# Agent attention and gated feed-forward in one kernel: fixed places for the values, denser keys, a column for eps

## The chip, the cores and the metric

The kernel runs on one core of a Trainium2 chip. The metric is the device time of one execution in microseconds. Engines: TensorE (PE, matmuls; PEld is its weight load), VectorE (DVE), ScalarE (ACT), GpSimd (POOL) and SyncE (SP), which here issues all DMA transfers. Each engine works through its own queue in order and waits on semaphores.

## The reference

```python
def _attn_ref(q, k, v, agents):            # B, N, C = 4, 12480, 128; 49 agents
    scale = 1.0 / np.sqrt(q.shape[-1])
    def sm(a, b):
        s = scale * (a @ b.transpose(0, 2, 1))
        s = s - s.max(-1, keepdims=True)
        e = np.exp(s)
        return e / (e.sum(-1, keepdims=True) + 1e-09)
    a2k = sm(agents, k)
    agent_v = a2k @ v
    q2a = sm(q, agents)
    return (q2a @ agent_v).astype(np.float32)

def _moe_ref(x, w_in, w_out):              # 49920 tokens, 128 -> 2048 -> 128
    h = x @ w_in
    g = h * (1.0 / (1.0 + np.exp(-1.702 * h)))
    return (g @ w_out).astype(np.float32)
```

The output is `_moe_ref(_attn_ref(q, k, v, agents))`. In each batch 49 agents attend to 12480 keys and collect values, the 12480 queries attend to the agents, and each token's result goes through a feed-forward layer with a hidden width of 2048.

## The kernel before, in words

**Two parts.** For a batch the kernel first works out `agent_v` and folds it into the first feed-forward matrix: `avT` times `w_in` gives weights `wh`, `wl` (high and low part) of 128 by 2048, of which the agents fill the rows (`weights_sums`, `weights_part`). After that a token needs only its softmax over the agents, the *pairs* `sa`, `sb` (a high and a low part stacked), as the moving operand of the up matmuls.

**Steps and groups.** A group is 960 tokens (2 halves of 480); a batch has 13 groups, four batches 52. A group takes NF = 16 steps, one for each 128 of the hidden width, so there are 832 steps. In step t = 16 n + f:

- `up` makes four matmuls of 480 columns (L386, L388) into two PSUM banks of a ring of four, and ScalarE applies the gated activation to both halves (L391) into `g`;
- the jobs that are listed for this step, below;
- `high_low` makes `gh` (L398 on ScalarE for the steps in HI_ON_ACT, L400 on VectorE for the other eight) and `gl` = g - gh (L401, VectorE);
- `down` makes six matmuls (L412) of step t - LAG, LAG = 4, from `gh` and `gl` of that step into `po`; after step 15 of a group `store` copies `po` (L423) and sends it out.

So TensorE is at step t while `gl` of t - 4 is the latest that it needs.

**Jobs.** A table `at` holds for every step the functions to run there, in the order in which `put` was called. For the query group n + 1, during group n: scores at step Q_AT = 4 (32 small matmuls L177 to L180, reduced by VectorE at L184), shift by the maximum at 5 (L341, L342), exponential at E_AT = 7 (ScalarE, with a table load before and after), sums at 9 (L351 reduce, L352 adds eps, L353 reciprocal), softmax at 10 (L358), transposes and pairs at P_AT = 13 (L369, L374 to L377); the load of group n + 2 at 5 and its split into three bf16 parts on GpSimd (L163, L164) at S_AT = 14.

For the next batch, during this one, 13 key groups and 13 value groups:

- *keys*: load 13 steps ahead, split 6 ahead (GpSimd, L163 and L164), scores at step t (as for a query; `score` holds them), partial maximum at t + 1 (L223). They come every 6 steps in the first batch, every 7 in the others. Then the maximum over all keys (`key_max_0` to `key_max_2`, two transposes on TensorE);
- *values*: subtract the maximum (GpSimd, L263), exponential with the query's at step 7 of some group (L267), two or three key groups at a time; at t - 2 `key_pair` (ScalarE L272, GpSimd L273) and `value_hi` (VectorE L276); at t - 1 `value_lo` (VectorE L280); at t eight matmuls `key_values` (L284); at t + 1 VectorE adds the result (L301). They come every 7 steps;
- *weights*: sums, then four parts (L324 to L326).

`pe_step` moves a job of TensorE to the next step that holds none. All these small jobs share a ring of two PSUM buffers, `ps_m`: a third one waits until the first has been read.

**Order.** The steps run inside `tc.manual_schedule` for TensorE, ScalarE, VectorE and GpSimd: on these engines the instructions stand in the order of the program. What lies before the loop (all of the first batch's keys and values, the conversion of the first weights) is ordered by the scheduler. In group 0 the last three quarters of `w_out` are still converted from 64-bit words (`down_weights`, L119 to L141) at steps 1, 5 and 9.

```python
        slot = next(t for t in range(shift + 3, steps) if t % NF == E_AT)
        t = slot + 3
        for k in range(NKG):
            t = pe_step(t)
            ...
            put(t - 2, lambda k=k: key_pair(k))
            put(t - 2, lambda b=b, k=k: value_hi(k, vts[b + 1, k]))
            put(t - 1, lambda b=b, k=k: value_lo(k, vts.pop((b + 1, k))))
            put(t, lambda b=b, k=k: do_key_values(b + 1, k))
            put(t + 1, lambda b=b, k=k: do_key_sum(b + 1, k))
            last, t = t, t + 7
```

Of the kernel before, what the change touches and what calls it, by code (L numbers as in the profile page):

```python
# [8 lines left out]
F32 = mybir.dt.float32  # L9
F32R = mybir.dt.float32r  # L10
# [7 lines left out]
P = 128  # L18
TB = 120
# [3 lines left out]
LAG = 4  # L23
RED = 1
PAD = 8
SD = 2
Q_AT = 4
E_AT = 7
P_AT = 13
S_AT = 14  # L30
FIRST_WORDS = (1, 3, 5, 7)
FIRST_UP = (0, 2, 4, 6)
HI_ON_ACT = (0, 2, 5, 6, 10, 12, 13, 14)
EPS = 1e-09


# [1 line left out]
def kernel(  # L38
# [47 lines left out]
    for i in range(2):  # L86
# [7 lines left out]
        nc.gpsimd.memset(t, 0.0)  # L94
        p_pad.append(t)

    w_in_sb = const.tile([P, F], F32, name="w_in_sb")
    wo_h = const.tile([P, NF, C], F32R, name="wo_h")
    wo_l = const.tile([P, NF, C], F32R, name="wo_l")
# [47 lines left out]
    for i in range(3):  # L147
        nc.vector.tensor_copy(out=ag_part[:, :, i, :], in_=rest)
        if i < 2:
            ag_rest = work.tile([P, B, A], F32, name="ag_rest", tag="sd", bufs=SD)  # L150
            nc.vector.tensor_sub(out=ag_rest, in0=rest, in1=ag_part[:, :, i, :])
            rest = ag_rest

# [177 lines left out]
        nc.sync.dma_start(out=t[:, 0:GT], in_=qT[b, :, g * GT : (g + 1) * GT])  # L331
        return t

    def query_scores(b, parts):
        sd = work.tile([P, KB, A], F32, name="sd", bufs=SD)
        scores(b, parts, sd[:TB])
        return sd

    def query_shift(sd):
        m = work.tile([P, KB], F32, name="m")  # L340
        nc.vector.tensor_reduce(out=m[:TB], in_=sd[:TB], axis=AX.X, op=ALU.max)  # L341
        nc.vector.tensor_tensor(  # L342
            out=sd[:TB], in0=sd[:TB], in1=m[:TB].unsqueeze(2).broadcast_to([TB, KB, A]), op=ALU.subtract
        )

    def query_exp(e):
        nc.scalar.activation(out=e[:TB], in_=e[:TB], func=AF.Exp, scale=scale)

    def query_sums(e):
        z = work.tile([P, KB], F32, name="z")  # L350
        nc.vector.tensor_reduce(out=z[:TB], in_=e[:TB], axis=AX.X, op=ALU.add)  # L351
        nc.vector.tensor_scalar_add(out=z[:TB], in0=z[:TB], scalar1=EPS)  # L352
        nc.vector.reciprocal(out=z[:TB], in_=z[:TB])  # L353
        return z

    def query_softmax(g, e, z):
        pp = p_pad[g % 2]
        nc.vector.tensor_tensor(  # L358
            out=pp[:TB].rearrange("p i (c x) -> p c i x", c=2)[:, :, :, 0:A],
            in0=e[:TB].rearrange("p (c i) a -> p c i a", c=2),  # L360
            in1=z[:TB].rearrange("p (c i) -> p c i", c=2).unsqueeze(3).broadcast_to([TB, 2, KB // 2, A]),
            op=ALU.mult,
        )
# [17 lines left out]
    def up(f, wts, pairs):  # L381
        wh, wl = wts
        s = slice(f * P, (f + 1) * P)
        ph = [ps_h.tile([P, 512], F32, name="ph") for _ in range(2)]
        for c in range(2):
            nc.tensor.matmul(out=ph[c][:, :CH], lhsT=wh[:, s], rhs=pairs[c], start=True, stop=False)  # L386
        for c in range(2):
            nc.tensor.matmul(out=ph[c][:, :CH], lhsT=wl[:, s], rhs=pairs[c], start=False, stop=True)  # L388
        g = gpool.tile([P, 2, CH], F32, name="g")
        for c in range(2):  # L390
            nc.scalar.activation(out=g[:, c, :], in_=ph[c][:, :CH], func=AF.Gelu_apprx_sigmoid)  # L391
        return g

    def high_low(f, g):
        gh = gpool.tile([P, 2, CH], F32R, name="gh", bufs=LAG + 1)
        gl = gpool.tile([P, 2, CH], F32R, name="gl", bufs=LAG + 1)
        if f in HI_ON_ACT:
            nc.scalar.copy(out=gh, in_=g)  # L398
        else:
            nc.vector.tensor_copy(out=gh, in_=g)  # L400
        nc.vector.tensor_sub(out=gl, in0=g, in1=gh.bitcast(F32))  # L401
        return gh, gl
# [66 lines left out]
    def do_query_scores(n):  # L469
        if n < B * NG:  # L470
            b, g = divmod(n, NG)
            scored[n] = query_scores(b, q_parts.pop(n))

    def do_query_shift(n):
        if n < B * NG:
# [5 lines left out]

    def do_query_sums(n):
        if n < B * NG:
            sums[n] = query_sums(scored[n])

    def do_query_softmax(n):
        if n < B * NG:
# [6 lines left out]


    def first_keys():
        tags = [("g", 3), ("gh", LAG + 1), ("gl", LAG + 1)]
# [129 lines left out]
    E = mybir.EngineType  # L627
    live = {}
    po = {}
    with tc.manual_schedule(engines={E.PE, E.Activation, E.DVE, E.Pool}):  # L630
        for t in range(steps + LAG):
            if t < steps:
                n, f = divmod(t, NF)
                g = up(f, wts[n // NG], pairs[n])
                if f == NF - 1:
                    pairs.pop(n)
            for job in at.pop(t, ()):
                job()
            if t < steps:
                live[t] = high_low(f, g)  # L640
            if t >= LAG:
                n, f = divmod(t - LAG, NF)
                if f == 0:
                    po[n] = [ps_o.tile([P, 512], F32, name=f"po{c}") for c in range(2)]
                down(f, live.pop(t - LAG), po[n])
                if f == NF - 1:
                    store(*divmod(n, NG), po.pop(n))
    assert not at


# [36 lines left out]
```

## Time and profile before

| | us |
|---|---|
| median of 3 runs | 2275.52 |
| lowest and highest run | 2273.99, 2277.99 |
| the profiled execution | 2273.38 |
| its span, first to last instruction | 2271.6 |

The mean granted clock of TensorE in the span was 0.972 of full speed. In rows of groups the columns are: line, engine, operation, output and inputs, shapes, count, then busy time, mean ns of one, and the idle time before them with what ended it. In rows of the timeline: start and duration in us, engine, line, operation, and in brackets the engine's idle time before with its releaser. In rows of waits: engine and line, what it waited for, us in total, times, longest. In rows by stretch: the stretch and its length, then for PE, PEld, DVE, ACT and POOL the busy time with the count of instructions, the granted clock, the share of the DMA engines and GB/s.

### The profile page before, as it was taken

Reading aid. Unit: us, or ns where it says so; the run is one execution under the profiler, and the core shown is the slowest. Engines: PE = TensorE matmul, PEld = TensorE weight load, DVE = VectorE, ACT = ScalarE, POOL = GpSimd, SP = SyncE. Lnnn points to the kernel's source line nnn. Section 1 sums busy time; section 2 is a strip of 40 time slices with the busy share of each in tenths; the row PEclk is TensorE's granted clock in tenths of the full one; section 3 lists DMA queues with packets and bytes.
Section 4 is the critical chain, followed back from the end, with each engine's and each line's share of the span. In section 5 each row is a group of like instructions: output and inputs, shape, how many; then the busy total and the mean of one; then the engine's idle time right before and its main releaser. Section 6 shows DMA issues by size and latency. Waiting matters only on the chain.

```text
span 2271.6 us, 31765 instructions
## 1 busy us (share of the span) xinstructions
PE 2126.4 (94%) x12232; PEld 1810.4 (80%) x12232; DVE 1918.7 (84%) x2142; ACT 1578.6 (69%) x2560; POOL 530.3 (23%) x383
## 2 busy tenths in 40 slices
PE   8789988897999999898899999989889999999999
PEld 8578877776788888776778888877677888888887
DVE  6799988877889999878788999978778888888876
ACT  3377766675677777666667777766576878787876
POOL 3144322211213333232122333232212101111000
PEclk9899999999999999999999999999999999999999
DMA  9312111211111111111111111111110010101000
GB/s 259 95 53 68 49 42 35 61 35 44 44 36 53 53 54 44 53 44 35 44 44 44 44 62 53 46 43 44 44 35 28 26 33 21 36 18 36 18 18 18
DMA packets 49339, 108.57 MB, mean 48 GB/s; under 512 B 4252, under 2 KB 30172, under 8 KB 49188
## 3 DMA queue, kind: packets, MB, share of 16 engines
q1 hardware_dynamic: 49188, 106.55, 15.9%
q8 instruction: 96, 1.57, 0.3%
q14 instruction: 55, 0.45, 0.1%
HBM read 80.97 MB, written 25.56 MB: 47 GB/s over the span
## 4 chain that ended last, share of the span: by engine, by line
PE 75%; DVE 16%; ACT 5%; issue 3%; DMA 1%; POOL 0%; ACTq 0%; SPq 0%; DVEq 0%; POOLq 0%
PE po L412 40%; PE ph L386 13%; PE ph L388 13%; DVE gl L401 6%; DVE v_pair L280 3%; PE ps_m L284 3%; DVE gh L400 3%; ACT g L391 2%; ACT gh L398 1%; PE ps_m L177 1%; PE ps_m L200 1%; PE ps_m L179 1%; PE ps_m L369 1%; PE ps_m L324 1%; PE ps_m L178 1%
## 5 line engine op out<-in xcount | busy, mean ns | idle before, releaser
L391 ACT ACTIVATE g<-ph 128x480 f32<-128x480 f32 x1664 | 855.6, 571 | 569.3 <-PE ph L388 494.0
L401 DVE TENSOR_TENSOR gl<-g,gh 128x960 fp32r<-128x960 f32 x832 | 1096.2, 1323 | 179.7 <-ACT gh L398 162.0
L412 PE MATMUL po<-gh,wo_h 128*128 128x480 f32 x1664 | 525.9, 398 | 0.0
L412 PE MATMUL po<-gh,wo_l 128*128 128x480 f32 x1664 | 507.7, 387 | 0.0
L412 PE MATMUL po<-gl,wo_h 128*128 128x480 f32 x1664 | 506.1, 386 | 0.0
L398 ACT CAST gh<-g 128x960 fp32r<-128x960 f32 x416 | 415.0, 997 | 12.2
L400 DVE CAST gh<-g 128x960 fp32r<-128x960 f32 x416 | 334.8, 805 | 74.0 <-ACT g L391 73.4
L412 PEld LDWEIGHTS po<-gl,wo_h 128*128 128x128 f32 x1664 | 319.6, 192 | 52.6
L412 PEld LDWEIGHTS po<-gh,wo_l 128*128 128x128 f32 x1664 | 318.9, 192 | 51.4
L412 PEld LDWEIGHTS po<-gh,wo_h 128*128 128x128 f32 x1664 | 304.9, 193 | 44.8 <-issue 5.7
L386 PE MATMUL ph<-sa,wh 128*128 128x480 f32 x832 | 321.2, 386 | 10.6 <-ACT g L391 10.5
L386 PE MATMUL ph<-sb,wh 128*128 128x480 f32 x832 | 320.1, 385 | 0.5 <-ACT g L391 0.5
L388 PE MATMUL ph<-sa,wl 128*128 128x480 f32 x832 | 318.7, 383 | 0.0
L388 PE MATMUL ph<-sb,wl 128*128 128x480 f32 x832 | 316.8, 381 | 0.0
L164 POOL TENSOR_TENSOR rest<-rest 128x968 bf16<-128x968 f32 x91 | 215.8, 2372 | 7.1
L386 PEld LDWEIGHTS ph<-sa,wh 128*128 128x128 f32 x832 | 159.3, 192 | 43.6 <-ACT g L391 15.5
L273 POOL TENSOR_TENSOR e_pair<-score,e_pair 120x392 fp32r<-120x392 f32 x39 | 42.1, 1079 | 640.8 <-ACT e_pair L272 591.2
L386 PEld LDWEIGHTS ph<-sb,wh 128*128 128x128 f32 x832 | 158.5, 190 | 32.1 <-ACT g L391 5.3
L388 PEld LDWEIGHTS ph<-sb,wl 128*128 128x128 f32 x832 | 157.3, 189 | 25.9 <-issue 0.2
L388 PEld LDWEIGHTS ph<-sa,wl 128*128 128x128 f32 x832 | 157.5, 189 | 25.2 <-issue 0.5
L163 POOL TENSOR_TENSOR rest<-kt 128x968 f32<-128x968 f32 x39 | 78.5, 2013 | 375.8 <-issue 360.5
L284 PE MATMUL ps_m<-v_pair,e_pair 120*128 120x258 f32 x312 | 60.3, 350 | 101.2 <-DVE v_pair L280 100.7
(102 smaller groups left out, 2059.3 us busy)
## 6 DMA issues: line engine op xcount, KB each, us to landing
kt<-kT SPq DMA_DIRECT2D x52, 480.0 KB, 3.5
qt<-qT SPq DMA_DIRECT2D x52, 480.0 KB, 3.6
vt<-v SPq DMA_DIRECT2D x52, 480.0 KB, 4.3
outT<-o SPq DMA_DIRECT2D x104, 240.0 KB, 2.1
words<-w_in SPq DMA_DIRECT2D x4, 512.0 KB, 11.6
words<-w_out SPq DMA_DIRECT2D x4, 512.0 KB, 8.1
ag_sb<-agT SPq DMA_DIRECT2D x1, 98.0 KB, 2.0
```

The costliest lines, as they stand in the source:

```text
L163: nc.gpsimd.tensor_sub(out=r, in0=t, in1=halves(t)[0])
L164: nc.gpsimd.tensor_sub(out=halves(r)[1], in0=r, in1=halves(r)[0])
L273: nc.gpsimd.tensor_sub(out=ep[:TB, :, H : H + A], in0=sc, in1=ep[:TB, :, 0:A].bitcast(F32))
L280: nc.vector.tensor_sub(out=vp[:TB, :, C : 2 * C], in0=vt[:TB], in1=vp[:TB, :, 0:C].bitcast(F32))
L284: nc.tensor.matmul(out=ps[:, : 2 * C + 2], lhsT=e_pair[g % 2][:TB, j, :], rhs=v_pair[g % 2][:TB, j, :], start=(first and j == 0), stop=(la ...
L386: nc.tensor.matmul(out=ph[c][:, :CH], lhsT=wh[:, s], rhs=pairs[c], start=True, stop=False)
L388: nc.tensor.matmul(out=ph[c][:, :CH], lhsT=wl[:, s], rhs=pairs[c], start=False, stop=True)
L391: nc.scalar.activation(out=g[:, c, :], in_=ph[c][:, :CH], func=AF.Gelu_apprx_sigmoid)
L398: nc.scalar.copy(out=gh, in_=g)
L400: nc.vector.tensor_copy(out=gh, in_=g)
L401: nc.vector.tensor_sub(out=gl, in0=g, in1=gh.bitcast(F32))
L412: nc.tensor.matmul(out=po[c][:, :CH], lhsT=lhsT[:, f, :], rhs=rhs[:, c, :], start=(f == 0 and first), stop=(f == NF - 1 and last),)
```

## The change

- *Values at two places.* They no longer come every seven steps but at steps 3 (V_AT) and 12 (V2_AT) of a group, two a group. `value_hi` and `value_lo` both move to four steps ahead of the matmuls, `key_pair` to three; the load goes 16 ahead (from 14). The exponentials are taken for two key groups at a time.
- *Keys every five steps* in all batches, from step 16 of the first and from step 4 of the others (before: 16 and 6); their split 5 steps ahead; loads of the later batches may start in the batch before.
- *Eps as a column.* The query's scores lie in two fixed tiles `e_sb` with a 50th column that holds eps, so that the sum over 50 columns has it; L352 goes.
- *Buffers.* `g` has four (three before), `gl` four (five before). Steps whose high half is made on ScalarE: 15 in place of 13.
- *Group 0.* The loop's body becomes `step(t)`; the first 16 steps run outside `manual_schedule`.

```diff
+K_AT = 4
+V_AT = 3
+V2_AT = 12
-HI_ON_ACT = (0, 2, 5, 6, 10, 12, 13, 14)
+HI_ON_ACT = (0, 2, 5, 6, 10, 12, 14, 15)
...
+    e_sb = []
+    for i in range(2):
+        t = const.tile([P, KB, A + 1], F32, name=f"e_sb{i}")
+        nc.gpsimd.memset(t[:, :, A:], EPS)
+        e_sb.append(t)
...
-    def query_scores(b, parts):
-        sd = work.tile([P, KB, A], F32, name="sd", bufs=SD)
-        scores(b, parts, sd[:TB])
+    def query_scores(n, b, parts):
+        sd = e_sb[n % 2][:TB, :, 0:A]
+        scores(b, parts, sd)
         return sd
...
-    def query_sums(e):
+    def query_sums(n):
         z = work.tile([P, KB], F32, name="z")
-        nc.vector.tensor_reduce(out=z[:TB], in_=e[:TB], axis=AX.X, op=ALU.add)
-        nc.vector.tensor_scalar_add(out=z[:TB], in0=z[:TB], scalar1=EPS)
+        nc.vector.tensor_reduce(out=z[:TB], in_=e_sb[n % 2][:TB], axis=AX.X, op=ALU.add)
         nc.vector.reciprocal(out=z[:TB], in_=z[:TB])
...
-        g = gpool.tile([P, 2, CH], F32, name="g")
+        g = gpool.tile([P, 2, CH], F32, name="g", bufs=LAG)
...
-        gl = gpool.tile([P, 2, CH], F32R, name="gl", bufs=LAG + 1)
+        gl = gpool.tile([P, 2, CH], F32R, name="gl", bufs=LAG)
...
-        first, apart = (16, 6) if b == 0 else (6, 7)
         for k in range(NKG):
-            t = pe_step(s0 + first + apart * k)
-            put(max(t - 13, s0), lambda b=b, k=k: do_key_load(b + 1, k))
-            put(max(t - 6, s0), lambda b=b, k=k: do_key_split(b + 1, k))
+            t = pe_step(s0 + (NF if b == 0 else K_AT) + 5 * k)
+            put(t - 13 if b else max(t - 13, 0), lambda b=b, k=k: do_key_load(b + 1, k))
+            put(max(t - 5, s0), lambda b=b, k=k: do_key_split(b + 1, k))
...
-        slot = next(t for t in range(shift + 3, steps) if t % NF == E_AT)
-        t = slot + 3
+        g0 = (shift + 2 - s0 - E_AT + NF - 1) // NF
         for k in range(NKG):
-            t = pe_step(t)
-            while t > slot + NF + 5:
-                slot += NF
+            g = g0 + (k + 1) // 2
+            slot = s0 + (g0 + k // 2) * NF + E_AT
             exps.setdefault(slot, []).append(k)
+            t = s0 + g * NF + (V_AT if k % 2 else V2_AT)
...
-            put(t - 14, lambda b=b, k=k: do_value_load(b + 1, k))
-            put(t - 2, lambda k=k: key_pair(k))
-            put(t - 2, lambda b=b, k=k: value_hi(k, vts[b + 1, k]))
-            put(t - 1, lambda b=b, k=k: value_lo(k, vts.pop((b + 1, k))))
+            put(t - 16, lambda b=b, k=k: do_value_load(b + 1, k))
+            put(t - 3, lambda k=k: key_pair(k))
+            put(t - 4, lambda b=b, k=k: value_hi(k, vts[b + 1, k]))
+            put(t - 4, lambda b=b, k=k: value_lo(k, vts.pop((b + 1, k))))
...
-            last, t = t, t + 7
+            last = t
...
+    def step(t):
...
+    for t in range(NF):
+        step(t)
     with tc.manual_schedule(engines={E.PE, E.Activation, E.DVE, E.Pool}):
-        for t in range(steps + LAG):
...
+        for t in range(NF, steps + LAG):
+            step(t)
```

More of the change, by code (lines that the diff above doesn't have):

```diff
@@ L25 @@
 PAD = 8
-SD = 2
 Q_AT = 4
@@ L149 @@
         if i < 2:
-            ag_rest = work.tile([P, B, A], F32, name="ag_rest", tag="sd", bufs=SD)
+            ag_rest = work.tile([P, B, A], F32, name="ag_rest")
             nc.vector.tensor_sub(out=ag_rest, in0=rest, in1=ag_part[:, :, i, :])
@@ L340, in query_shift, with query_softmax @@
         m = work.tile([P, KB], F32, name="m")
-        nc.vector.tensor_reduce(out=m[:TB], in_=sd[:TB], axis=AX.X, op=ALU.max)
+        nc.vector.tensor_reduce(out=m[:TB], in_=sd, axis=AX.X, op=ALU.max)
         nc.vector.tensor_tensor(
-            out=sd[:TB], in0=sd[:TB], in1=m[:TB].unsqueeze(2).broadcast_to([TB, KB, A]), op=ALU.subtract
+            out=sd, in0=sd, in1=m[:TB].unsqueeze(2).broadcast_to([TB, KB, A]), op=ALU.subtract
         )
     def query_exp(e):
-        nc.scalar.activation(out=e[:TB], in_=e[:TB], func=AF.Exp, scale=scale)
-    def query_sums(e):
+        nc.scalar.activation(out=e, in_=e, func=AF.Exp, scale=scale)
+    def query_sums(n):
         z = work.tile([P, KB], F32, name="z")
-        nc.vector.tensor_reduce(out=z[:TB], in_=e[:TB], axis=AX.X, op=ALU.add)
-        nc.vector.tensor_scalar_add(out=z[:TB], in0=z[:TB], scalar1=EPS)
+        nc.vector.tensor_reduce(out=z[:TB], in_=e_sb[n % 2][:TB], axis=AX.X, op=ALU.add)
         nc.vector.reciprocal(out=z[:TB], in_=z[:TB])
         return z
-    def query_softmax(g, e, z):
-        pp = p_pad[g % 2]
+    def query_softmax(n, e, z):
+        pp = p_pad[n % 2]
         nc.vector.tensor_tensor(
             out=pp[:TB].rearrange("p i (c x) -> p c i x", c=2)[:, :, :, 0:A],
-            in0=e[:TB].rearrange("p (c i) a -> p c i a", c=2),
+            in0=e.rearrange("p (c i) a -> p c i a", c=2),
             in1=z[:TB].rearrange("p (c i) -> p c i", c=2).unsqueeze(3).broadcast_to([TB, 2, KB // 2, A]),
@@ L471, in do_query_scores @@
             b, g = divmod(n, NG)
-            scored[n] = query_scores(b, q_parts.pop(n))
+            scored[n] = query_scores(n, b, q_parts.pop(n))
     def do_query_shift(n):
@@ L483, in do_query_sums @@
         if n < B * NG:
-            sums[n] = query_sums(scored[n])
+            sums[n] = query_sums(n)
     def do_query_softmax(n):
@@ L496, in first_keys @@
     def first_keys():
-        tags = [("g", 3), ("gh", LAG + 1), ("gl", LAG + 1)]
+        tags = [("g", LAG), ("gh", LAG + 1), ("gl", LAG)]
         tiles = []
@@ L589 @@
         shift = t + 2
-        slot = next(t for t in range(shift + 3, steps) if t % NF == E_AT)
-        t = slot + 3
+        g0 = (shift + 2 - s0 - E_AT + NF - 1) // NF
         for k in range(NKG):
-            t = pe_step(t)
-            while t > slot + NF + 5:
-                slot += NF
+            g = g0 + (k + 1) // 2
+            slot = s0 + (g0 + k // 2) * NF + E_AT
             exps.setdefault(slot, []).append(k)
+            t = s0 + g * NF + (V_AT if k % 2 else V2_AT)
             put(min(shift + 3 * k, slot - 1), lambda k=k: key_shift(k, nc.gpsimd.tensor_tensor))
-            put(t - 14, lambda b=b, k=k: do_value_load(b + 1, k))
-            put(t - 2, lambda k=k: key_pair(k))
-            put(t - 2, lambda b=b, k=k: value_hi(k, vts[b + 1, k]))
-            put(t - 1, lambda b=b, k=k: value_lo(k, vts.pop((b + 1, k))))
+            put(t - 16, lambda b=b, k=k: do_value_load(b + 1, k))
+            put(t - 3, lambda k=k: key_pair(k))
+            put(t - 4, lambda b=b, k=k: value_hi(k, vts[b + 1, k]))
+            put(t - 4, lambda b=b, k=k: value_lo(k, vts.pop((b + 1, k))))
+            assert t not in pe_steps
             put(t, lambda b=b, k=k: do_key_values(b + 1, k))
             put(t + 1, lambda b=b, k=k: do_key_sum(b + 1, k))
-            last, t = t, t + 7
+            last = t
         w = {}
@@ L629 @@
     po = {}
-    with tc.manual_schedule(engines={E.PE, E.Activation, E.DVE, E.Pool}):
-        for t in range(steps + LAG):
[L632 to L647, printed above, removed]
+    def step(t):
+        if t < steps:
+            n, f = divmod(t, NF)
+            g = up(f, wts[n // NG], pairs[n])
+            if f == NF - 1:
+                pairs.pop(n)
+        for job in at.pop(t, ()):
+            job()
+        if t < steps:
+            live[t] = high_low(f, g)
+        if t >= LAG:
+            n, f = divmod(t - LAG, NF)
+            if f == 0:
+                po[n] = [ps_o.tile([P, 512], F32, name=f"po{c}") for c in range(2)]
+            down(f, live.pop(t - LAG), po[n])
+            if f == NF - 1:
+                store(*divmod(n, NG), po.pop(n))
+    for t in range(NF):
+        step(t)
+    with tc.manual_schedule(engines={E.PE, E.Activation, E.DVE, E.Pool}):
+        for t in range(NF, steps + LAG):
+            step(t)
     assert not at
```

## The prediction, made before the run

> **What bounds the kernel now.** I read the page's engine rows first, then busy time by stretches of groups, the chain of waits, and the timeline round single steps.
>
> ```profile
> span 2271.6 us, 31765 instructions
> ...
> PE 2126.4 (94%) x12232; PEld 1810.4 (80%) x12232; DVE 1918.7 (84%) x2142; ACT 1578.6 (69%) x2560; POOL 530.3 (23%) x383
> ```
>
> TensorE is busy for 94%, but with modelled ends that says little. A group of 16 steps, alone, is seen in the last batch, where no keys or values are prepared: the output copies of two neighbouring groups in the timeline.
>
> ```profile
> 1869.44 1.02 ACT L423 COPY o<-po 128x480 f32<-128x480 f32 x2 [0.28 <-PE po L412]
> ...
> 1906.08 1.03 ACT L423 COPY o<-po 128x480 f32<-128x480 f32 x2 [0.27 <-PE po L412]
> ```
>
> 1906.08 - 1869.44 = 36.64 us a group. Now busy time in stretches, in order: group 0; the keys of batch 1 (groups 1 to 5); its values and weights (6 to 12); keys and values of batch 2 (13 to 18, 19 to 25) and of batch 3 (26 to 31, 32 to 38); and ten bare groups.
>
> ```profile
> 74.24:127.42 53.18, 40.10 (x179) 29.88 (x178) 45.24 (x62) 30.75 (x50) 8.05 (x7) 0.91 0.13 37
> 127.42:339.47 212.05, 203.13 (x1400) 173.11 (x1398) 200.22 (x215) 148.49 (x238) 76.99 (x52) 0.98 0.18 54
> 339.47:664.45 324.98, 290.53 (x1491) 245.10 (x1490) 262.63 (x286) 216.47 (x352) 69.26 (x50) 0.95 0.14 42
> 664.45:900.52 236.07, 235.87 (x1594) 202.36 (x1593) 223.76 (x247) 176.23 (x282) 79.88 (x53) 1.00 0.18 53
> 900.52:1227.44 326.92, 292.51 (x1493) 246.19 (x1491) 263.80 (x287) 216.51 (x352) 71.80 (x51) 0.94 0.14 41
> 1227.44:1463.63 236.19, 236.00 (x1594) 202.70 (x1593) 223.93 (x247) 176.27 (x282) 79.68 (x53) 1.00 0.18 53
> 1463.63:1787.45 323.82, 289.35 (x1492) 243.89 (x1491) 262.07 (x287) 216.50 (x352) 72.67 (x50) 0.96 0.13 37
> 1824.09:2190.42 366.33, 366.33 (x1961) 314.95 (x1960) 304.10 (x341) 293.14 (x470) 41.40 (x27) 1.00 0.08 26
> ```
>
> After the length come PE, PEld, DVE, ACT and POOL, then the granted clock. Ten bare groups take 366.33 (36.63 each) at clock 1.00, with VectorE busy for 30.41 a group. Where values are prepared the clock is 0.94 to 0.96 and TensorE idles. To say how much is lost I need the bare price of a key (a query's scores are the same 32 matmuls), of a value, and of the weights:
>
> ```profile
> 1906.98 0.22 PE L177 MATMUL ps_m<-ag_part,qt 128*128 128x98 bf16 x1
> ...
> 1908.12 0.68 PE L412 MATMUL po<-gh,wo_h 128*128 128x480 f32 x2
> ```
> ```profile
> 1721.72 1.20 PE L284 MATMUL ps_m<-v_pair,e_pair 120*128 120x258 f32 x8 [0.26 <-DVE v_pair L280]
> ...
> 1722.76 0.60 PE L412 MATMUL po<-gh,wo_h 128*128 128x480 f32 x2
> ```
> ```profile
> L324 PE MATMUL ps_m<-w_in_sb,avT 128*128 128x512 f32 x32 | 18.4, 666 | 3.7 <-DVE avT L315 3.7
> ```
>
> A key costs 1908.12 - 1906.98 = 1.14, a value 1722.76 - 1721.72 = 1.04, the weights of a batch 18.4 / 4 = 4.6. So the three value stretches (975.72) hold 21 x 36.63 + 39 x 1.04 + 3 x 4.6 = 823.6 of work: **152.1 lost**. The key stretches lose 212.05 - 5 x 36.63 - 13 x 1.14 = 14.1, then 1.5 and 1.6; group 0 loses 53.18 - 36.63 = 16.6. Together 185.9; with none of it the span would be 2271.6 - 185.9 = 2085.7.
>
> Who makes TensorE wait:
>
> ```profile
> PEld ps_m L284 <- issue: 115.9, 39, 6.9
> PE ps_m L284 <- DVE v_pair L280: 100.7, 36, 6.5
> ...
> ACT wo_h L140 <- DVE m L131: 30.5, 4, 17.2
> ...
> ACT g L391 <- DVE gl L401: 25.8, 14, 4.4
> ...
> PE ps_m L369 <- DVE score L184: 6.2, 2, 4.7
> ```
>
> The value matmuls wait 36 of 39 times for the low half that VectorE makes one step before (L280). One of the worst, first on VectorE, then on TensorE:
>
> ```profile
> 1068.92 0.66 DVE L400 CAST gh<-g 128x960 fp32r<-128x960 f32 x1 [3.08 <-ACT g L391]
> ...
> 1074.70 2.64 DVE L401 TENSOR_TENSOR gl<-g,gh 128x960 fp32r<-128x960 f32 x1
> 1077.26 0.68 DVE L276 CAST v_pair<-vt 120x1024 fp32r<-120x1024 f32 x1
> ...
> 1078.34 1.15 DVE L401 TENSOR_TENSOR gl<-g,gh 128x960 fp32r<-128x960 f32 x1
> 1079.41 1.21 DVE L280 TENSOR_TENSOR v_pair<-vt,v_pair 120x1024 fp32r<-120x1024 f32 x1
> ```
> ```profile
> 1080.77 2.06 PE L284 MATMUL ps_m<-v_pair,e_pair 120*128 120x258 f32 x8 [6.52 <-DVE v_pair L280]
> 1082.62 1.00 PE L412 MATMUL po<-gh,wo_h 128*128 128x480 f32 x2
> ```
>
> VectorE is in order. The down matmuls run four steps behind, so it may be four steps late; L280, put one step ahead, stands behind the gl of two steps before, and TensorE gives up nearly all that slack. After the 6.52 us gap two down matmuls take 1.00 instead of 0.60: the wait is paid again in clock.
>
> **The change, part by part.** *Values.* L276 and L280 move four steps ahead. At step t they now stand behind gl of step t - 5, and the down matmuls of step t need gl of t - 4 anyhow: TensorE waits no longer for them than it would for that. They go to steps 15 and 8; step 8 lies in the gap that ScalarE's exponentials leave on VectorE (the 3.08 us above). The key pair (ScalarE copy, GpSimd subtraction) goes from two to three steps ahead; behind it on GpSimd stand only key shifts and the query split of step 14, which is needed six steps later. VectorE's demand in a value group: (263.80 - 7 x 30.41) / 13 = 3.9 a value, with shifts and weights; 30.4 + 2 x 3.9 = 38.2 against TensorE's 36.63 + 2 x 1.04 = 38.7. It fits, with 1% to spare. What is late next: at step 4 the query scores need two PSUM buffers of a ring of two, and one is held by the value of step 3 until VectorE has added it (L301), behind gl of step 3; and at step 10 TensorE meets ScalarE's backlog after two exponentials. Bounds: 0.26 us a value (the best now, L284 at 1721.72) and the 152.1 / 39 = 3.9 of today. With VectorE just under demand I take nearer to the best, 0.75 a value: 10 a batch, **30**. The weights' sums now come two steps after the last value and wait for its addition; as now, +1.3 a batch, **4**.
>
> *Keys every five steps* (from six and seven): the same work in 65 steps. Rows for a key, which VectorE and GpSimd share:
>
> ```profile
> L164 POOL TENSOR_TENSOR rest<-rest 128x968 bf16<-128x968 f32 x91 | 215.8, 2372 | 7.1
> ...
> L163 POOL TENSOR_TENSOR rest<-kt 128x968 f32<-128x968 f32 x39 | 78.5, 2013 | 375.8 <-issue 360.5
> ...
> L184 DVE TENSOR_REDUCE score<-ps_m 120x196 f32<-120x392 f32 x78 | 40.4, 557 | 0.5
> ...
> L223 DVE TENSOR_REDUCE part_max<-score 120x49 f32<-120x392 f32 x39 | 33.4, 856 | 0.0
> ...
> L352 DVE TENSOR_SCALAR z<-z 120x8 f32<-120x8 f32 x52 | 18.6, 358 | 1.8
> ```
>
> A key's own VectorE work is 2 x 0.557 + 0.856 = 1.97; measured between seven steps it is (223.76 - 6 x 30.41) / 13 = 3.18, the rest being time in which GpSimd's split holds VectorE up:
>
> ```profile
> 265.28 2.10 POOL L164 TENSOR_TENSOR rest<-rest 128x968 bf16<-128x968 f32 x1
> ...
> 265.75 2.64 DVE L401 TENSOR_TENSOR gl<-g,gh 128x960 fp32r<-128x960 f32 x1
> ```
>
> (2.64 for a gl that takes 1.15 free.) At 16 / 5 = 3.2 keys a group VectorE needs 30.41 - 0.36 + 3.2 x 3.18 = 40.2, TensorE 36.63 + 3.2 x 1.14 = 40.3: level, with four steps of slack to start from, so it falls behind late. Bounds of the loss: 1.5 a batch (seven steps) and, by the six-step stretch, 14.1 or more. I take 14 for batch 1 as now, and 8 for each of the others, of which some 3 are the key maximum's transposes, which now fall beside the query scores at step 4 and wait for VectorE's reduction: **30**. A key at step 12 beside the pairs at 13 (batch 1 and 2) can wait like the 4.7 of L369 above; that is in the 14.
>
> The Trainium skill, "SBUF — State Buffer", section "Who interferes with whom", speaks against this part: a VectorE instruction with two SBUF inputs and a GpSimd one that reads SBUF share an exclusive lock, and the second waits for the whole first. By it every split could cost its full length; the trace at seven steps shows less (3.18, not the 6.35 worked out below as a rival).
>
> *Eps as a column* drops L352, 18.6 us of VectorE in all, 0.36 a group, already counted; the sum over 50 instead of 49 columns adds some 10 ns each. Its two small GpSimd memsets fall in the start, where that engine is idle. Nothing by itself on the path. *Rings*: g four deep instead of three lets ScalarE run on (at most its 25.8 of waits for gl); gl four instead of five makes gl of step t wait for the down matmuls of the same step, which only binds a VectorE that is early. *High half of step 13 to VectorE, of 15 to ScalarE*: one for one, zero; it lightens step 15, where value work now stands. *Loads*: values 16 steps ahead (from 14), keys 13 ahead and split 5 ahead (from 6), for transfers that land in
>
> ```profile
> kt<-kT SPq DMA_DIRECT2D x52, 480.0 KB, 3.5
> ...
> vt<-v SPq DMA_DIRECT2D x52, 480.0 KB, 4.3
> ```
>
> 4 us: eight steps of 2.2 hide them, also on SyncE's in-order queue, where outputs and query loads stand behind them.
>
> *Group 0 left to the scheduler.* Today ScalarE stands at the cast of the down weights until VectorE has converted them, and activations queue behind it:
>
> ```profile
> 87.04 0.62 ACT L140 CAST wo_h<-m 128x512 fp32r<-128x512 f32 x1 [4.41 <-DVE m L131]
> ...
> 114.44 0.62 ACT L140 CAST wo_h<-m 128x512 fp32r<-128x512 f32 x1 [5.10 <-DVE m L131]
> ```
>
> A reordering can win up to the 16.6 that the group loses, or lose as much; VectorE's 45.24 of work in it remains. I take a loss of **12** left.
>
> Sum: 2085.7 + 30 + 4 + 30 + 12 = 2161.7 span. The profiled run took 2273.38, 1.8 more than its span, and lies 2.1 below the median 2275.52. Prediction 2163 us, about 5% less.
>
> **Rivals.** (1) *Nothing but the work is left in the values and keys*: values at 0.26 each (10), weights 4, keys as at seven steps (14.1 + 3.1), group 0 at 6: 2085.7 + 37 + 1.8 = 2125. For it: the 3.08 gap at step 8; against it: VectorE is level with TensorE.
> (2) *The waits only move*: half of the 152.1 comes back at step 4 and step 13, where PSUM's ring of two makes TensorE wait for VectorE. 76 instead of 30: 2209, and with group 0 and keys worse too about 2220. For it: L369 waited 4.7 in just that way; against: only 2 times.
> (3) *Slower, through the key stretches*: every split holds VectorE for its whole length, 1.97 + 2.01 + 2.37 = 6.35 a key. Then VectorE needs 30.05 + 3.2 x 6.35 = 50.4 a group against 40.3: 10.1 x 65 / 16 x 3 = 123 us, 3.2 a key. Gaps of that length also cost clock, as after L284; at the 1.0 to 1.7 that a doubled stretch of matmuls adds, 39 x 4.5 = 176. Without its key term of 30 my sum is 2133.5, so 2310. It decides from 138 / 39 = 3.5 us a key. This is what the Trainium skill's page on SBUF gives in full. Against: at seven steps the rule would make VectorE need 30.4 + 2.29 x 6.35 = 44.9 a group, and 236.07 / 6 = 39.3 was measured.
> (4) *No effect*: within 0.2% (4.5 us, about what a measurement of this kernel can tell from no change), if each wait saved on L280 reappears on gl.
>
> **How the numbers follow.** Forecast 0.58 (2135 to 2195), rival 1 0.17, rival 2 0.18, rival 3 0.04, rival 4 0.03. Faster 0.93, same 0.03, slower 0.04. The range leaves out 3 and 4 and the ends of 1 and 2: 2110 to 2222.
>
> **What would show it.** Value matmuls that wait for L280 a few us in all instead of 100.7; granted clock 0.98 or more in value groups of 39 to 41 us (now 46); key groups of 40 to 42; no tensor_scalar on z. Wrong if the waits of pairs, query scores or L412 on VectorE grow to tens of us, if key groups pass 43, or if group 0 takes over 60.

## The result, and the profile after

| | before | after |
|---|---|---|
| median, us | 2274.76 (4 runs, 2273.01 to 2277.99) | 2211.57 (4 runs, 2210.20 to 2212.38) |
| the profiled execution, its span, us | 2273.38, 2271.6 | 2211.75, 2209.6 |

The ratio is 0.972, with a 95% interval of 0.9703 to 0.9737: 63 us faster. The forecast was 2163 us, in a range of 2110 to 2222.

The engine rows of the changed kernel's page, for the same rows of before:

```profile
span 2209.6 us, 32197 instructions
...
PE 2102.9 (95%) x12232; PEld 1795.3 (81%) x12232; DVE 1913.1 (87%) x2090; ACT 1579.7 (71%) x2563; POOL 552.4 (25%) x385
```

VectorE has 52 instructions fewer (the adding of eps) and almost the same busy time. The stretches, cut where the work now changes: group 0; the keys of batch 1 (groups 1 to 4); its values and weights (5 to 12); keys (13 to 17) and values (18 to 25) of batch 2; the same of batch 3; ten bare groups:

```profile
73.57:117.49 43.92, 37.77 (x174) 29.14 (x173) 42.83 (x59) 29.96 (x49) 9.51 (x6) 0.90 0.16 46
117.49:292.71 175.22, 167.09 (x1206) 142.21 (x1205) 166.78 (x178) 120.47 (x192) 74.50 (x47) 0.98 0.20 60
292.71:632.27 339.56, 319.88 (x1689) 271.64 (x1687) 291.63 (x312) 244.34 (x400) 80.52 (x54) 0.97 0.14 43
632.27:844.73 212.46, 203.15 (x1400) 173.06 (x1398) 198.74 (x208) 147.63 (x236) 86.54 (x56) 0.98 0.18 54
844.73:1179.31 334.58, 317.88 (x1687) 270.30 (x1686) 290.03 (x313) 245.08 (x401) 70.39 (x48) 0.98 0.14 43
1179.31:1391.61 212.30, 203.07 (x1400) 173.52 (x1398) 198.68 (x208) 147.66 (x236) 86.52 (x56) 0.98 0.18 54
1391.61:1725.59 333.98, 316.83 (x1688) 269.72 (x1687) 290.43 (x313) 245.09 (x401) 71.07 (x47) 0.98 0.13 39
1762.21:2128.30 366.09, 366.09 (x1961) 314.85 (x1960) 300.64 (x331) 294.22 (x471) 43.05 (x27) 1.00 0.08 26
```

With the prediction's bare prices (a group 36.63, a key 1.14, a value 1.04, a batch's weights 4.6) the losses after are these. Values and weights: 1008.12 in 24 groups, less 24 x 36.63 + 39 x 1.04 + 13.8 = 933.5, so **74.6** (before 152.1). Keys: 175.22 - 4 x 36.63 - 14.8 = 13.9, then with five groups each 14.5 and 14.3, so **42.7** (before 17.2). Group 0: **7.3** (before 16.6). Together 124.6, and 2085.7 + 124.6 = 2210.3 is the span to within 1 us. So the values gave back half of their loss, and the keys took a third of that away.

TensorE's waits, the five longest (engine and line, what it waited for, us in total, times, longest):

```profile
PE ps_m L186 <- DVE acc L310: 30.3, 18, 3.9
PE ps_m L317 <- DVE acc L310: 13.7, 3, 4.6
PE ps_m L377 <- DVE score L193: 12.8, 5, 3.6
PE ps_m L186 <- DVE sb L385: 10.2, 7, 1.9
PE ps_m L319 <- DVE zc L316: 6.4, 3, 2.1
```

The wait for the second rounding of the values (100.7 us) is gone. All the new ones are for a PSUM buffer of the ring of two, or for what VectorE makes of one: query scores and key scores (L186) wait for the addition of a value (L310) or for a pair (L385), pairs (L377) for a reduction (L193), the weights' sums (L317, L319) for the last addition. The question was why VectorE is late there. One place is step 14 of the last value group, 11.9 us long instead of 2.2 (a step's length here goes from the start of its up matmuls to that of the next). GpSimd, VectorE and TensorE in the timeline of the changed kernel:

```profile
1116.30 1.37 POOL L282 TENSOR_TENSOR e_pair<-score,e_pair 120x392 fp32r<-120x392 f32 x1 [22.76 <-ACT e_pair L281]
...
1117.79 2.08 POOL L172 TENSOR_TENSOR rest<-qt 128x968 f32<-128x968 f32 x1
1119.95 2.60 POOL L173 TENSOR_TENSOR rest<-rest 128x968 bf16<-128x968 f32 x1
...
1122.67 1.96 POOL L172 TENSOR_TENSOR rest<-qt 128x968 f32<-128x968 f32 x1
1124.71 2.60 POOL L173 TENSOR_TENSOR rest<-rest 128x968 bf16<-128x968 f32 x1
```
```profile
1115.67 1.16 DVE L409 TENSOR_TENSOR gl<-g,gh 128x960 fp32r<-128x960 f32 x1
...
1118.32 2.56 DVE L409 TENSOR_TENSOR gl<-g,gh 128x960 fp32r<-128x960 f32 x1
1120.81 2.16 DVE L366 TENSOR_TENSOR p_pad<-e_sb,z 120x392 f32<-120x392 f32 x1
1122.89 2.75 DVE L409 TENSOR_TENSOR gl<-g,gh 128x960 fp32r<-128x960 f32 x1
1125.56 2.29 DVE L408 CAST gh<-g 128x960 fp32r<-128x960 f32 x1
...
1130.10 0.42 DVE L310 TENSOR_TENSOR acc<-ps_m,acc 128x257 f32<-128x257 f32 x1
```
```profile
1130.67 0.77 PE L317 MATMUL ps_m<-sel,acc 128*128 128x128 f32 x2 [4.54 <-DVE acc L310]
...
1134.01 0.80 PE L319 MATMUL ps_m<-sel,zc 128*128 128x128 f32 x2 [2.14 <-DVE zc L316]
1134.46 1.15 PE L420 MATMUL po<-gh,wo_h 128*128 128x480 f32 x2
```

Two query splits run in a row. They are listed for step 14 of this group and of the next, but GpSimd is held only by its order and its inputs: behind the last key pair nothing stops it, so it is at work from step 11 on, where VectorE also has softmax and pairs to make. While they run, a gl takes 2.56 and 2.75 instead of 1.16, the softmax product 2.16 (0.56 where GpSimd rests), a rounding 2.29 (0.65). VectorE is some 6 us late, TensorE stands for 4.54 + 2.14, and then works at half speed (1.15 for two matmuls that take 0.60). None of TensorE's waits is for a split itself.

The other place is step 4 of the first groups with a value at step 3 (6, 7, 19 and 32), 8.6 to 9.1 us instead of 3.4. There it is three key shifts in a row. GpSimd and then TensorE in group 19:

```profile
886.27 1.48 POOL L282 TENSOR_TENSOR e_pair<-score,e_pair 120x392 fp32r<-120x392 f32 x1 [6.17 <-ACT e_pair L281]
887.70 5.16 POOL L272 TENSOR_TENSOR score<-score,max_b 120x392 f32<-120x392 f32 x3
```
```profile
899.11 0.26 PE L186 MATMUL ps_m<-ag_part,qt 128*128 128x98 bf16 x1 [3.90 <-DVE acc L310]
```

### The profile page after: what moved, and what is told of

The parts are those of the page before. It is cut to its first block, busy times and chain, and to the rows that moved or that the text cites. A ratio compares the mean times of both kernels' runs of the same rounds, so it can differ in the third digit from the quotient of the medians.

```text
span 2209.6 us, 32197 instructions
## 1 busy us (share of the span) xinstructions
PE 2102.9 (95%) x12232; PEld 1795.3 (81%) x12232; DVE 1913.1 (87%) x2090; ACT 1579.7 (71%) x2563; POOL 552.4 (25%) x385
## 4 chain that ended last, share of the span: by engine, by line
PE 76%; DVE 17%; issue 5%; ACT 1%; DMA 1%; POOL 0%; DVEq 0%; ACTq 0%; SPq 0%; POOLq 0%
PE po L420 41%; PE ph L394 14%; PE ph L396 13%; DVE gl L409 8%; DVE gh L408 3%; PE ps_m L186 1%; PE ps_m L209 1%; PE ps_m L188 1%; PE ps_m L293 1%; DVE p_pad L366 1%; PE ps_m L377 1%; PE ps_m L333 1%; DVE sb L385 1%; DVE sa L384 1%; PE ps_m L187 1%
## 5 line engine op out<-in xcount | busy, mean ns | idle before, releaser
L408 DVE CAST gh<-g 128x960 fp32r<-128x960 f32 x416 | 322.6, 776 | 39.7 <-ACT g L399 37.9
L282 POOL TENSOR_TENSOR e_pair<-score,e_pair 120x392 fp32r<-120x392 f32 x39 | 54.3, 1392 | 651.9 <-ACT e_pair L281 651.9
L172 POOL TENSOR_TENSOR rest<-qt 128x968 f32<-128x968 f32 x52 | 112.2, 2159 | 194.3 <-issue 115.2
L172 POOL TENSOR_TENSOR rest<-kt 128x968 f32<-128x968 f32 x39 | 86.3, 2214 | 259.7 <-issue 247.4
```

The source lines that it names most:

```text
L172: nc.gpsimd.tensor_sub(out=r, in0=t, in1=halves(t)[0])
L282: nc.gpsimd.tensor_sub(out=ep[:TB, :, H : H + A], in0=sc, in1=ep[:TB, :, 0:A].bitcast(F32))
```

## The experiments

The theory that these rows suggest: TensorE loses time where one of its jobs needs VectorE's result within a step or three, and VectorE is late because GpSimd, which runs ahead of the steps, works in its busy stretches. The main rival: VectorE is late because of its own work, more of it per group since the keys and values are denser.

| kernel | median, us | ratio to before, 95% interval |
|---|---|---|
| the change | 2211.57 | 0.9703 to 0.9737 |
| weights_late | 2196.91 | 0.9649 to 0.9678 |
| shifts_early | 2209.98 | 0.9694 to 0.9734 |
| keys_placed | 2207.81 | 0.9697 to 0.9726 |
| keys_six | 2219.63 | 0.9750 to 0.9779 |
| values_near | 2371.23 | 1.0412 to 1.0443 |
| group0_manual | 2220.04 | 0.9747 to 0.9778 |
| no_third | 2146.90 | 0.9425 to 0.9453 |
| split_gated | 2158.54 | 0.9478 to 0.9511 |
| split_six | 2219.38 | 0.9734 to 0.9760 |
| gated_late | 2150.98 | 0.9438 to 0.9464 |
| gated_hi_act | 2134.18 | 0.9363 to 0.9388 |
| all_shown | 2117.24 | 0.9300 to 0.9326 |

The kernel before was run again beside each set, with medians of 2272.73 to 2276.42; ratios are to those. All edits below are against the changed kernel.

**values_near: the lead undone, the places kept.**

```diff
-            put(t - 3, lambda k=k: key_pair(k))
-            put(t - 4, ... value_hi ...)
-            put(t - 4, ... value_lo ...)
+            put(t - 2, lambda k=k: key_pair(k))
+            put(t - 2, ... value_hi ...)
+            put(t - 1, ... value_lo ...)
```

> The pair of a key, and the first rounding of its values, are put two steps ahead of the value matmuls again and the second rounding one step ahead, as before the change; the two fixed places a group, the key spacing, the column for eps and the first group stay as changed. Theory (the lead is what pays): the wait for the second rounding of the values, none in the changed kernel, is back at some 3 to 4 us for each of 36 value blocks, so 100 to 130 us more than the changed kernel, 2290 to 2340 us. Rival (the fixed places pay, the lead adds little): under 30 us more, 2211 to 2240 us.

160 us more than with the lead, above the range expected, and 97 more than the kernel before the change. TensorE's waits of values_near, the first row:

```profile
PE ps_m L293 <- DVE v_pair L289: 171.0, 39, 9.4
```

At these places the lead is what pays. The fixed places without it are worse than the old ones: the value at step 12 now makes that step 11 to 14 us long in every value group, since its second rounding, listed for step 11, falls where the split runs (steps 11 and 12). The lead at the old seven steps was not run, so how the two parts share the gain is not shown.

**group0_manual: the first 16 steps back in the written order.**

```diff
-    for t in range(NF):
+    for t in range(0):
         step(t)
     with tc.manual_schedule(engines={E.PE, E.Activation, E.DVE, E.Pool}):
-        for t in range(NF, steps + LAG):
+        for t in range(steps + LAG):
```

> The first 16 steps go back into the order written out by hand; all else as changed. Theory: the first group takes its old 53 us instead of 43.9, so the time is 8 to 10 us more than the changed kernel's, 2219 to 2222 us. Rival (the changed split of roundings between ScalarE and VectorE and the later keys shorten the first group, not the scheduler): the first group stays at 43 to 46 us and the time at 2210 to 2213 us.

As the theory says: 8.5 us more. ScalarE's waits in group 0 (of this kernel, then of the changed one) show what the scheduler takes away:

```profile
ACT wo_h L149 <- DVE m L140: 13.6, 3, 5.2
```
```profile
ACT wo_h L149 <- DVE m L140: 0.9, 1, 0.9
```

**weights_late: the weights' sums five steps after the last value, not two.**

```diff
-        put(pe_step(last + 2), lambda b=b, w=w: weights_sums(accs.pop(b + 1), w))
-        t = last + 3
+        put(pe_step(last + 5), lambda b=b, w=w: weights_sums(accs.pop(b + 1), w))
+        t = last + 6
```

> The weights' sums go from two to five steps after the last value (from step 14 to step 1 of the next group), the four parts three steps later; nothing else. Theory (sync points): in the changed kernel TensorE waits 4.5 and 2.1 us there because VectorE has just been held by two query splits of GpSimd in a row and stands four steps back; three steps later it has caught up. The three steps of 11.9 to 12.0 us fall to 2.2, the sums cost about 3.7 at their new place as they did in the kernel before: 3 x 8 = 24 us less, about 2187 (2183 to 2193). Rival (demand): VectorE has as much to do as TensorE, so lateness is only carried to the next point where TensorE waits; less than 8 us saved, 2204 to 2212.

14.7 us less, between the two expectations. Step 14 falls from 11.9 to 2.2 us, and half of that, some 5 us a batch, comes back in the next four steps. At most 1.6 of it are the sums' own matmuls; for the rest TensorE meets the same late VectorE in another place.

**shifts_early: all 13 key shifts of batches 2 and 3 listed ahead of the first pair.**

```diff
-            put(min(shift + 3 * k, slot - 1), ... key_shift ...)
+            put(shift if b else min(shift + 3 * k, slot - 1), ... key_shift ...)
```

> In batches 2 and 3 all 13 key shifts are put at the step where the maximum is known, ahead of the first key pair on GpSimd's queue; batch 1 stays as it is. Theory (sync points): the 9.1 us of step 4 in groups 19 and 32 come from three shifts in a row that GpSimd does in steps 1 to 3, behind the key pair; they fall to 4.5 to 5.3 as in the groups after them, while steps 4 of groups 6 and 7 (8.6 and 8.9) stay. 8 to 12 us less with the next groups' carry, of which 2 to 4 come back in groups 17 and 18: about 2205. Rival (demand): the same lock time costs the same in groups 17 and 18: 2210 to 2213.

No more than 1.6 us, within the intervals, as the rival said. Groups 19 and 20 gain 7.0 us, since step 4 of group 19 falls from 9.1 to 4.5; groups 17 and 18, where the shifts now run, lose 5.3. GpSimd's work was only moved from one busy stretch into another.

**keys_placed and keys_six: other steps for the keys of batches 2 and 3.** In the first they stand at fixed steps 6, 10 and 0, three a group; in the second every six steps instead of five.

```diff
-            t = pe_step(s0 + (NF if b == 0 else K_AT) + 5 * k)
+            t = pe_step(s0 + (NF + 5 * k if b == 0 else 6 + (0, 4, 10)[k % 3] + NF * (k // 3)))
```
```diff
-            t = pe_step(s0 + (NF if b == 0 else K_AT) + 5 * k)
+            t = pe_step(s0 + (NF + 5 * k if b == 0 else K_AT + 6 * k))
```

> In batches 2 and 3 the keys stand at steps 0, 6 and 10 of a group (three a group, 13 keys in 64 steps as in the changed kernel), away from the pairs at 13 and the query scores at 4; batch 1 stays. Theory (ring of two): TensorE's transposes of the pairs at step 13 wait for a PSUM buffer that VectorE still has to reduce for the key of step 11 or 12 (7.2, 6.3, 7.9, 6.7 us steps), and keys at 14 wait for the pairs (5.1, 5.2). These go: 16 to 24 us less, 2188 to 2196. Rival (density): VectorE's demand of 40 us a group is what costs, wherever the keys stand: key groups stay at 42 to 45, 2206 to 2213.

> In batches 2 and 3 the keys come every six steps instead of five (from the same first step), values at the same places; keys fall on step 12 twice and on 14 once. Density: key groups fall to 39 to 40 and the loss of 14 us a batch to 3: 2188 to 2192, better than placing the keys. Ring of two: the two keys at step 12 still make the pairs wait 2 to 5 us each, the one at 14 about 1.5: a loss of 7 to 10 a batch stays, 2200 to 2206.

Neither did what it was built for. At fixed steps the pairs at step 13 wait for the softmax instead of for a key's reduction. The key groups of the two batches take 9.3 us less together, but the value groups behind them 4.8 more, and the 3.8 us between the medians lie within the intervals. Their rows of TensorE's waits, keys_placed and then keys_six:

```profile
PE ps_m L377 <- DVE p_pad L366: 11.8, 10, 2.0
```
```profile
PE ps_m L377 <- DVE score L193: 14.8, 5, 5.2
```

Every six steps is 8 us *slower*, though it asks less of VectorE per group. The key groups don't lose it: those of batch 2 take 211.1 us instead of 212.5, those of batch 3 as much as before, since step 13 behind a key at step 12 takes 9.4 us in two of them and 4.7 in two. Groups 20 and 33 lose it, 9.7 us together. The maximum over the keys is known later, so three key shifts in a row now stand in a second value group, and step 4 there grows from 5.3 to 9.0 and 8.6 us. GpSimd at step 1 of group 20:

```profile
929.64 1.46 POOL L282 TENSOR_TENSOR e_pair<-score,e_pair 120x392 fp32r<-120x392 f32 x1 [6.94 <-ACT e_pair L281]
931.06 5.14 POOL L272 TENSOR_TENSOR score<-score,max_b 120x392 f32<-120x392 f32 x3
```

So neither the ring of two alone nor the density alone explains the keys, and the run with fewer keys a group lost its time to GpSimd in the value groups. VectorE is late at step 13 with and without a key beside it.

**no_third: less work for GpSimd, none for the others.** The kernel leaves out the third part of each split: the second part is used twice, so the scores have other low bits.

```diff
-        nc.gpsimd.tensor_sub(out=halves(r)[1], in0=r, in1=halves(r)[0])
-        return halves(t)[0], halves(r)[0], halves(r)[1]
+        return halves(t)[0], halves(r)[0], halves(r)[0]
```

> Leaves out the second subtraction of each split of keys and of queries on GpSimd (91 of some 2.4 us), the third part of a split being the second one again, so scores have other low bits. No other engine's work changes. Theory (TensorE loses its time where VectorE is late, and VectorE is late because GpSimd holds what the two share during the splits): key groups lose 4 us a batch instead of 14, step 14 of each last value group 6 us or less instead of 11.9, together 30 to 45 us less than the changed kernel, 2165 to 2180 us. Rival (VectorE is late by its own work): GpSimd's load doesn't matter and the time stays above 2200 us.

64.7 us less, more than the theory asked for, with nothing taken off VectorE's own list. The keys give some 30 of it, values and weights as much, group 0 the other 5. The key and value stretches of batch 2:

```profile
609.77:810.46 200.69, 199.58 (x1399) 170.83 (x1398) 178.99 (x209) 147.31 (x236) 43.56 (x39) 1.00 0.19 58
810.46:1135.69 325.23, 317.29 (x1687) 270.77 (x1686) 276.90 (x312) 244.98 (x401) 48.03 (x39) 0.98 0.15 45
```

The keys lose 2.7 us instead of 14.5, and VectorE is busy for 178.99 instead of 198.74 with the same instructions: some 20 us of its "busy" time were time in which GpSimd held it. What is left in the values stands behind the key shifts, which this edit does not touch, and at the weights' sums (step 14 still takes 8.7).

**split_gated: the split held to a gap of VectorE.** In the groups with values it stands at step 6 behind a copy of one column of the query maximum, which VectorE makes at step 5.

```diff
+                nc.gpsimd.tensor_copy(out=gate[:TB], in_=maxes[0][:TB, 0:1])
             q_parts[n] = split(qts.pop(n))
...
-        put(s0 + S_AT, lambda n=n: do_query_split(n + 2))
+        held = n < (B - 1) * NG and n % NG >= 5
+        put(s0 + (6 if held else S_AT), lambda n=n, held=held: do_query_split(n + 2, held))
```

> In the groups with values the query's split is put at step 6 instead of step 14, behind a copy of one number of the query's maximum on GpSimd, so that it can't run ahead of it, nor two splits in a row. Theory (two splits in a row at the last value group's step 14 are what makes VectorE late for the weights' sums): step 14 of those groups falls from 11.9 to about 5 us, and 15 to 25 us go, 2187 to 2196 us. Rival (the lateness only moves with the split, to the steps behind the scores): less than 5 us, 2207 to 2216 us.

53 us less, twice what was expected. Keys and values of batch 2:

```profile
610.94:823.46 212.52, 203.34 (x1400) 173.07 (x1398) 200.31 (x209) 147.63 (x236) 86.38 (x56) 0.98 0.18 54
823.46:1139.36 315.90, 311.73 (x1688) 266.14 (x1687) 286.52 (x312) 245.15 (x401) 77.98 (x56) 1.00 0.16 46
```

The values lose 315.90 - 311.2 = 4.7 us instead of 23.4, though GpSimd is busy for longer (77.98, was 70.39). The keys, whose splits are not held, are as before. GpSimd, then VectorE, in one such group:

```profile
994.74 0.58 POOL L468 COPY gate<-m 120x1 f32<-120x1 f32 x1 [10.84 <-DVE m L351]
...
995.44 1.80 POOL L172 TENSOR_TENSOR rest<-qt 128x968 f32<-128x968 f32 x1
997.32 2.60 POOL L173 TENSOR_TENSOR rest<-rest 128x968 bf16<-128x968 f32 x1
```
```profile
995.95 4.98 DVE L410 TENSOR_TENSOR gl<-g,gh 128x960 fp32r<-128x960 f32 x2 [0.68 <-ACT gh L407]
```

Two gl take 4.98 instead of 2.23: the split still costs VectorE 2.75 us. But here VectorE is ahead: in the same group of the changed kernel it stands idle for ScalarE before a gl or a rounding at steps 6, 7 and 10, for 0.68, 1.06 and 1.15 us. With the split at step 6 the last two of these idle times are gone, and VectorE has made the delay up before TensorE needs anything within a step.

**split_six: the same place without the hold.**

```diff
-        put(s0 + S_AT, lambda n=n: do_query_split(n + 2))
+        early = n < (B - 1) * NG and n % NG >= 5
+        put(s0 + (6 if early else S_AT), lambda n=n: do_query_split(n + 2))
```

> As the kernel with the held split, but nothing holds it: the query's split only stands at step 6 instead of step 14 in the order of GpSimd's instructions, in the groups with values. Theory (it is enough that a key pair, which can't run ahead, stands between two splits): the same time as with the hold, 2153 to 2164 us. Rival (the hold is what matters; without it the split starts behind the pair of step 0 and meets the query scores of step 4): step 4 stays at 4.5 us or more and the time is 2170 to 2200 us.

The rival is right, and by more than it said: 61 us slower than with the hold, and 8 slower than the changed kernel, at the edge of the intervals. GpSimd's timeline, then the longest of TensorE's waits:

```profile
1021.53 1.70 POOL L282 TENSOR_TENSOR e_pair<-score,e_pair 120x392 fp32r<-120x392 f32 x1 [14.01 <-ACT e_pair L281]
...
1023.35 2.55 POOL L172 TENSOR_TENSOR rest<-qt 128x968 f32<-128x968 f32 x1
```
```profile
PE ps_m L186 <- DVE acc L310: 49.8, 18, 5.8
```

A place in a table of steps is no time for an engine that nothing holds: the split starts straight behind the pair, two steps ahead of the query scores, and step 4 grows to 5.6 us and, in the first groups with a value there, to 10 or 11.

**gated_late and gated_hi_act.** Both hold the split. The first also has the late sums of weights_late; the second moves four roundings a group in the key groups of batches 2 and 3 to ScalarE:

```diff
-        if f in HI_ON_ACT:
+        if f in HI_ON_ACT or more and f in (3, 8, 11, 13):
...
-            live[t] = high_low(f, g)
+            live[t] = high_low(f, g, NG <= n < (B - 1) * NG and n % NG < 5)
```

> The held split together with the weights' sums three steps later. Theory (both shorten the wait at the weights' sums, 5.4 to 5.7 us at step 14 with the hold alone): that step falls to 2.2 us, 3.3 us for each of three batches, of which a part comes back in the next steps: 4 to 10 us less than with the hold alone, 2149 to 2155 us. Rival (with the splits apart, VectorE has caught up by the next steps and the lateness only moves with the sums): 2157 to 2160 us.

> The held split, and in the four groups with all keys of the second and third batch (eight groups) four more of the first roundings on ScalarE, which is busy two thirds of the time there, instead of VectorE, which is busy 95% of it. Theory (in key groups VectorE's own work, made longer by GpSimd's splits, is at its limit, so that whatever is taken from it comes off its lateness): 2.6 to 3.8 us of work go from each group; the groups of 45.6 and 44.5 us fall to about 41 us, 12 to 18 us less than with the hold alone, 2141 to 2147 us. Rival (only GpSimd's hold on what the two share counts; VectorE waits it out whatever it has to do): less than 4 us, 2155 to 2160 us.

The late sums bring 7.6 us, half of what they bring without the hold. The roundings bring 24.4, more than forecast. Keys of batch 2 in gated_hi_act:

```profile
610.28:810.50 200.22, 199.82 (x1400) 170.69 (x1399) 182.11 (x190) 165.42 (x256) 83.44 (x56) 1.00 0.19 58
```

The loss falls from 14.5 to 2.2 us with GpSimd nearly as busy (83.44, was 86.54). So in the key groups, where keys and queries are split and no gap is left to hide the splits in, both theories have a part: GpSimd's hold makes VectorE's work longer, and at 94% busy (198.74 of 212.46) it has nothing left to catch up with. Taking off either one, GpSimd's work or its own, is enough.

**all_shown: hold, late sums and roundings, these in the first batch's key groups too.**

```diff
-            live[t] = high_low(f, g, NG <= n < (B - 1) * NG and n % NG < 5)
+            live[t] = high_low(f, g, 0 < n < (B - 1) * NG and n % NG < 5)
```

> The held split, the weights' sums three steps later and the four roundings on ScalarE together, the last also in the groups 1 to 4 of the first batch. If the three losses are apart in time, the gains add: 2134 us with hold and roundings, less 7.6 us for the weights' sums, less 2 to 8 us for the first batch's key groups (43.2, 45.7, 42.0 and 44.1 us now, 40 to 42 us then): 2118 to 2126 us. Rival (the key groups of the first batch wait for their loads and not for VectorE, or the sums of the weights meet the roundings of the next key groups): 2126 to 2132 us.

2117.24 us, 0.9313 of before, just under the range expected: the gains add. Its page:

```profile
span 2111.9 us, 32188 instructions
...
PE 2074.4 (98%) x12232; PEld 1775.5 (84%) x12232; DVE 1845.9 (87%) x2034; ACT 1630.2 (77%) x2619; POOL 562.2 (27%) x409
```

Of the 124.6 us that the change left, 2111.9 - 2085.7 = 26.2 are left here.

## Why the prediction came out as it did

The time lies in the range, 49 us above the number and outside the likeliest case's own 2135 to 2195. It is the time of the second rival, "the waits only move" (2209), which had 0.18. That it meets the rival to some 2 us is luck in part: against the rival's terms, values and weights lose 5.4 less, keys 12.7 more and group 0 4.7 less. The rival also named only the ring of two, and not the engine that makes VectorE late.

*Values, 30 forecast.* The mechanism is as described: with the roundings four steps ahead the wait for them is gone, and without the lead it is back, and larger (171.0 us in values_near, 100.7 before). What comes next was named too, the ring of two at step 4 behind the addition of the value. Its size was not. The stretches lose 74.6 with the weights, where the second rival said 76 and 4 for the weights. The step that failed is "with VectorE just under demand I take nearer to the best, 0.75 a value". VectorE's demand was estimated well: (290.03 - 8 x 30.06) / 13 = 3.8 a value, 3.9 forecast. But an average over a group says nothing of the steps at which it is late, and the prediction put GpSimd's split at step 14, "needed six steps later", because the table says so. GpSimd was there from step 11 on. The row that could have shown it was in the fence on the worst wait: a gl of 2.64 just ahead of the late rounding, taken as VectorE's own delay though the same 2.64 was read as a split's doing for the keys. GpSimd's rows of the kernel before, at that moment, show a query split there too, at steps 11 and 12 of its group:

```profile
1072.35 1.80 POOL L163 TENSOR_TENSOR rest<-qt 128x968 f32<-128x968 f32 x1
1074.23 2.10 POOL L164 TENSOR_TENSOR rest<-rest 128x968 bf16<-128x968 f32 x1
```

With the split held, the values and weights of batch 2 lose 4.7 us, just the first rival's share (13 x 0.26 + 1.3).

*Weights' sums, 4 forecast.* The rows after show step 14 of three groups 9.7 us longer than an empty step. The sums' own matmuls are at most 1.6 of that (the step that holds them in gated_late takes 3.8 instead of the 2.2 of an empty one), so some 8 a batch, 24 in all: six times the term. The words "as now, +1.3 a batch" carried a price over to a place with two splits beside it.

*Keys, 30 forecast, 42.7 measured.* The prices of a key were taken from keys seven steps apart, 3.18 of VectorE. At five steps it is (198.74 - 5 x 30.06) / 13 = 3.73. The prediction's own row of keys six steps apart had nearly that: (200.22 - 5 x 30.41) / 13 = 3.71. So VectorE needs 30.06 + 3.2 x 3.73 = 42.0 a group against TensorE's 40.3: not level, but behind. That the loss stands at step 13, beside a key at step 12, was forecast. The third rival's full price, 6.35 a key, is refuted at this density too. (Its "3.5 us a key" set a time against a span; the median 2275.52 less 2133.5 gives 3.6.)

*Group 0, 12 forecast, 7.3 measured*, and the cause as given: ScalarE waits 0.9 us for the conversion, against 13.6 in group0_manual.

*Eps, 0.36 of VectorE a group forecast.* A bare group takes 30.06 of VectorE, 30.41 before, and TensorE's 36.6 is the same: right, and worth nothing by itself. The rings, the other two roundings and the loads were not tried alone; none of the waits above names them.

Of the signs that the prediction named, the first held (no wait for L289) and the clock nearly did (0.97 to 0.98). Value groups of 39 to 41 us came in most cases, but not in the first one or two of a batch (44.8 to 46.1) and the last with values (49.4 to 50.3); full key groups took 42 us five times in twelve and 43 to 46 otherwise. Two signs of an error came true: key groups over 43, and waits of query scores that grow to tens of us, here 30.3.

What stays open: groups 6 and 7 and groups 19 and 32, the first with a value at step 3, still lose 1 to 4 us each in all_shown, beside the key shifts. No run held those back, so that the shifts cause this is read from the timeline and from shifts_early and keys_six, where the loss moves with them.

## What to carry to other kernels

A step in a written order is a time only for an engine that something holds to it. For each engine with slack, read in the trace when its work really runs and which other engine it slows there; a one-column copy that waits on the right event can move it into a gap, and was worth nearly as much here as the whole change. When an engine's busy time is read as demand, check first whether the same instruction is shorter elsewhere in the trace.

## What the runs showed of the hardware

In the changed kernel a gl on VectorE, two inputs from SBUF, takes 1.16 us alone and up to 2.80 beside GpSimd's subtractions, which themselves take 1.8 at the least and often 2.6; the rounding, one input, takes 0.65 and up to 2.29. Reductions are not touched: L193, from PSUM, takes 0.56 beside a split as elsewhere, and so do L360 (0.56) and L232 (0.86), which read SBUF. In the timeline of the changed kernel, GpSimd and then VectorE in a key group:

```profile
736.29 2.65 POOL L172 TENSOR_TENSOR rest<-kt 128x968 f32<-128x968 f32 x1 [3.20 <-issue]
```
```profile
737.67 0.56 DVE L193 TENSOR_REDUCE score<-ps_m 120x196 f32<-120x392 f32 x1
738.14 1.31 DVE L408 CAST gh<-g 128x960 fp32r<-128x960 f32 x1
739.56 2.57 DVE L409 TENSOR_TENSOR gl<-g,gh 128x960 fp32r<-128x960 f32 x1
```

The Trainium skill, "SBUF — State Buffer", section "Who interferes with whom", has the rule: whoever comes second waits for the whole instruction of the first, a reduction never does, a cast can. The trace agrees in the rows of step 14 above: the gl that starts at 1118.32 ends 1.01 us after the GpSimd subtraction of 1117.79 has, at 1119.87, and the gl of 1122.89 ends 1.01 after the subtraction of 1122.67. The prediction's weighing of that rule went by sums, where only the rest of GpSimd's instruction counts for the one that comes second, and so made it look weaker than it is. What it costs the kernel depends on the step at which it strikes, from next to nothing (split_gated) to some 8 us (the weights' sums).
